# Strided products begun in the prologue, and the weight conversions regrouped, in a fused attention and mixture-of-experts kernel

## The chip, the cores and the metric

The kernel runs on one core of one Trainium2 chip. The metric is the device time of one execution in microseconds (us); the figure for a kernel is the median over its runs. TensorE is called PE, VectorE DVE, ScalarE ACT, GpSimd POOL, and SyncE, which issues the loads, SP.

## The reference, cut to what matters

```python
# attention: 4 batches, 8 heads, 576 positions, head size 64
scores = (q @ k.T) / 8
# heads 0-3: the last 32 positions ("local"); heads 4-7: every 32nd position ("strided")
attn = softmax(where(mask, scores, -1e9)) ; x = attn @ v          # -> x: 2304 x 512
# dense layer
h = x @ w_in                                                      # 512 -> 2048
g = h * sigmoid(1.702 * h)
x = g @ w_out                                                     # 2048 -> 512
# eight experts, two for each token
top2 = two largest of (x @ w_gate + log1p(exp(x @ w_noise)) * noise)
out += weight * (relu(x @ w1[e]) @ w2[e])   for each e in top2
```

## The kernel before, in words

Every fp32 product is made of three: an operand is split into a rounded part ("hi") and its remainder ("lo"), and hi*hi, hi*lo and lo*hi are accumulated in one PSUM bank.

**Attention** is cut into groups. A strided group covers 126 or 72 reordered positions of two heads, a local group 192 positions of two heads. A group passes through all engines: scores on PE (L223 or L238), mask and row minimum on DVE (L186), exponentials on ACT (L191), sums and reciprocals on DVE (L195, L198), scaling on POOL (L200), transposes on PE (L251 or L256) and their copy on ACT (L252 or L257), the product with v on PE (L268 or L278), and last the split of the result into the hi part of `xt` on ACT (L208) and its lo part on DVE (L211).

**The prologue** is the loop that ends before the dense layer. Its step k (0 to 16) issues the scores, mask and exponentials of group k, the reciprocals of group k-1, the transposes of group k-3 and the products with v of group k-4. Groups 0 to 9 are the strided ones of batch 0, groups 10 to 13 the local ones that its first 384 tokens need. `warm` (L890) is a product of ones into a bank that is about to be written; its result is never read.

**The dense layer** runs in slices (c, fc): 384 tokens, 128 hidden units. Slices 0 to 7 are (0, 0) to (0, 7). Slice (c, fc) has a first product (`m1_l1`, L461 to L463: four blocks kc of the 512 inputs, three products each, into bank fc % 2), tanh on ACT (L466), a product on DVE (L470), a split (L475 on ACT, L477 on POOL or DVE), and a second product (`m1_l2`, L487 to L489, nine instructions) that is issued one slice later. Blocks kc 2 and 3 of `xt` come from the strided heads, 0 and 1 from the local ones. In slices 0 to 7 two further attention groups are worked on between the products.

**Conversions.** The weights come as raw 64-bit words, in halves called pieces here: (f, 0) is the half of block f that the first product reads, (f, 1) that of the second. Turning a piece into fp32 takes three DVE instructions (L422, L425, L429), a cast on ACT (L393) and a subtraction on POOL (L394). The cast and the subtraction come one slot after the DVE instructions (a prologue step, or half a slice, is a slot), and only when they have been issued does the load of piece (f+2, s) follow on SP, into the buffer that they free (`w_split` calls `w_raw`; all these loads pass through `chained`, L157, in one order). `CONVAT` lists the prologue steps that convert a piece; each slice converts one in its first half, and slices 0, 2, 4 and 6 one in the second half too (L988). A conversion's first instruction stands ahead of the mask of its step; in the prologue its temporary is PSUM bank 7, later the SBUF tile `cv`.

PE, ACT, DVE and POOL run their instructions in the order in which the code issues them (`manual_schedule`): an instruction that waits holds back all behind it on its engine.

Of the kernel before, what the change touches and what calls it, by code (L numbers as in the profile page):

```python
# [28 lines left out]
CH = 384  # L29
# [5 lines left out]
NG = -(-BAND // RPG)  # L35
# [20 lines left out]
HALFC = NFC // 2  # L56
FIRSTLD = 18
SMALLS = 18
CONVAT = (4, 6, 7, 9, 11, 13)
R_PP = R_LG + 16 * TPC  # L60

XA = (0, 1, 0, 2, 1, 0, 2, 1)
# [45 lines left out]
def tile_kernel(ctx, tc, attL, attS, wm1, wm2, wgn, noise, cst, lst0, out):  # L108
    nc = tc.nc
# [4 lines left out]
    PB = [psum.tile([128, 512], F32, tag=f"pb{i}", name=f"pb{i}") for i in range(8)]  # L114
# [15 lines left out]
    with ExitStack() as main, tc.manual_schedule(engines={mybir.EngineType.PE}):  # L130
# [12 lines left out]
        def third(i):  # L143
            return XT[:, :, :, CH * (i % 3):CH * (i % 3) + CH]

        X = [third(c) for c in range(NCHUNK)]
# [242 lines left out]
        def w_split():  # L389

            for fc, s, w32, o, n in SPLIT.pop(0):
                hi, lo = W1[fc, s]
                nc.scalar.copy(hi[:, o:o + n], w32)  # L393
                nc.gpsimd.tensor_sub(lo[:, o:o + n], w32, hi[:, o:o + n].bitcast(F32))  # L394
                if n < 512:
                    held.pop()
                else:
                    w_raw(fc + 2, s)
            w_small()
            SPLIT.append([])  # L400
            done.append(0)

        def w_step():
            left = 512
            while PIECES and left:
                fc, s, raw, o, n = PIECES[0]
                if n < 512:
                    if len(done) < born[0] + LATE:
                        return
                    born.pop(0)  # L410
                PIECES.pop(0)
                left -= n
                yield from w_bits(fc, s, raw, o, n, PB[7][:, :n].bitcast(I32) if INPS else None)
# [35 lines left out]
                    nc.scalar.mul(p, PB[2 + j], 0.5)  # L449
                PART.append(p)  # L450

        def m1_l1(c, fc, mid, conv, between=None):
            w = W1[fc, 0]
            ps = PB[fc % 2][:, :CH]
            for n, kc in enumerate((2, 3, 0, 1)):
                if n == 2:
                    mid()
                if n == 3 and (c, fc) == (0, 0):
                    finish(0, [5])
                a = slice(128 * kc, 128 * kc + 128)  # L460
                nc.tensor.matmul(ps, w[0][:, a], X[c][:, 0, kc, :], start=(n == 0), stop=False)  # L461
                nc.tensor.matmul(ps, w[0][:, a], X[c][:, 1, kc, :], start=False, stop=False)  # L462
                nc.tensor.matmul(ps, w[1][:, a], X[c][:, 0, kc, :], start=False, stop=(n == 3))  # L463
            t = tmp.tile([128, CH], F32, tag="th", name="th", bufs=1)
            g = tmp.tile([128, 2, CH], F32R, tag="g", name="g")
            nc.scalar.activation(t, ps, AF.Tanh, scale=0.851)  # L466
            next(conv, None)
            if between:
                between()
            nc.vector.scalar_tensor_tensor(t, t, 1.0, ps, op0=OP.add, op1=OP.mult)  # L470
            GT[c, fc] = g
            return t, g
# [410 lines left out]
        upto = [sum(map(len, parts[:k + 1])) for k in range(len(parts))]  # L883
        att = Attention(sum(parts, []), upto[1], upto[1])
# [4 lines left out]
        def warm(bank):  # L889
            nc.tensor.matmul(bank.rearrange("p (t d) -> p t d", d=128), ones,  # L890
                             ones[:, None, :].to_broadcast([128, 4, 128]), start=True, stop=True)
# [8 lines left out]
        w_raw(1, 0)  # L900
        w_raw(1, 1)
        k = 0
        while att.done < upto[0] - REM:
            conv = w_step() if k in CONVAT else iter(())
            next(conv, None)
            if k and not att.nc:
                warm(PB[att.na % 3])
            att.scores([0, 1, 2])
            next(conv, None)
            att.norms(conv, True)  # L910
            if att.done < att.nc:
                warm(PB[5 + att.done % 2])
            att.values([5, 6])
            if k in CONVAT and att.nc < att.ready:
                warm(PB[3 + att.nc % 2])
            att.transposes([3, 4])
            att.exps()
            att.load()
            next(conv, None)
            for _ in conv:  # L920
                pass
            w_split()
            k += 1
# [27 lines left out]
        def finish(c, bank=[7]):  # L951
            while att.done < upto[c]:
                att.exps()
                att.values([7])
                att.norms()
                att.transposes([6])

        seq = [(c, fc) for c, a, b in SEGS for fc in range(a, b)]
        for i, (c, fc) in enumerate(seq):
# [10 lines left out]
            conv = w_step()  # L970
# [14 lines left out]
            for _ in conv:  # L985
                pass
            w_split()
            conv = w_step() if i < HALFC and not i % 2 or i >= SMALLS else iter(())  # L988
            if i < HALFC:
                att.exps()  # L990
                next(conv, None)
# [80 lines left out]
        for h in range(H0, H1):  # L1072
            e, fc = divmod(h, NF2)
# [44 lines left out]
    with tc.tile_pool(name="ovf", bufs=1) as op:  # L1118
        n = nc.values_load(nrow[:, 0:1], min_val=0, max_val=NJ)  # L1119
        with tc.For_i(0, n, 1) as j:  # L1120
# [14 lines left out]
            w = op.tile([128, NF2, 1024], F32, name="ow")  # L1135
            nc.sync.dma_start(w, wm2[bass.ds(e8, NF2)].rearrange("f p n -> p f n"))
            for fc in range(NF2):
                ps = PB[fc % 2][:, :128]
# [79 lines left out]
```

## Time and profile before

| what | value |
|---|---|
| median of 3 runs | 970.48 us (970.12 to 972.08) |
| the profiled execution's own time | 970.01 us |
| its span, first to last instruction | 968.2 us |
| PE busy | 951.5 us (98%) |
| DVE busy | 523.8 us (54%) |
| ACT busy | 387.8 us (40%) |
| POOL busy | 217.2 us (22%) |

The span is 1.8 us shorter than the execution's own time; what lies around it is taken as fixed. The shares are means over stages: in the prologue (up to 35.15 us) and in the dense layer the engines are loaded quite differently, so that single stretches and the order of single instructions have to be read.

### The profile page before, as it was taken

What the parts mean: (1) busy time and instruction counts of PE and PEld (TensorE: products, weight loads), DVE (VectorE), ACT (ScalarE), POOL (GpSimd) and SP (SyncE); (2) the same over time, 40 slices, a digit from 0 to 9 for tenths busy, and PEclk for the clock granted to TensorE, in tenths of its full rate; (3) what the DMA queues carried; (4) which work ended last, traced back from release to release, by engine and by line L of the source; (5) the groups of instructions that cost most, each with busy time, mean ns of one, the idle gap of its engine ahead of it and who ended that gap; (6) DMA issues with size and microseconds to landing.
All of it is one profiled execution on the core that took longest, in us unless ns stands there. A gap on an engine that the chain in (4) does not pass through costs nothing. (4 is left out here: it accounts for less than half of the span.)

```text
span 968.2 us, 15951 instructions
## 1 busy us (share of the span) xinstructions
PE 951.5 (98%) x5706; PEld 839.4 (87%) x5706; DVE 523.8 (54%) x1519; ACT 387.8 (40%) x1031; POOL 217.2 (22%) x206
## 2 busy tenths in 40 slices
PE   8999999999999999999999999999999999999996
PEld 4788899898888889899898988888988989898994
DVE  6889865567645745632666343645546272635511
ACT  6875533244444444223354242333424242433411
POOL 3575231020200200020230512050402204050303
PEclk9999999999999999999999999999999999999998
DMA  9755511061333237301064258276684939576503
GB/s 337 258 191 183 176 60 55 1 134 45 57 102 102 67 69 235 132 1 67 6 198 135 39 141 213 84 178 170 150 216 106 237 117 207 145 174 174 107 1 53
DMA packets 83793, 123.93 MB, mean 128 GB/s; under 512 B 13488, under 2 KB 42800, under 8 KB 83696
## 3 DMA queue, kind: packets, MB, share of 16 engines
q1 hardware_dynamic: 73888, 102.92, 35.5%
q0 software_dynamic: 9824, 19.98, 11.1%
q8 instruction: 45, 0.74, 0.3%
q14 instruction: 36, 0.29, 0.1%
HBM read 93.33 MB, written 29.68 MB: 127 GB/s over the span
## 5 line engine op out<-in xcount | busy, mean ns | idle before, releaser
L832 DVE SCALAR_TENSOR_TENSOR ht<-pb,ht 128x352 fp32r<-128x352 f32 (+2 forms) x126 | 59.1, 472 | 166.8 <-ACT ht L831 166.8
L461 PE MATMUL pb<-xt,w 128*128 128x384 f32 x384 | 132.0, 344 | 0.0
L462 PE MATMUL pb<-xt,w 128*128 128x384 f32 x384 | 129.8, 338 | 0.0
L463 PE MATMUL pb<-xt,w 128*128 128x384 f32 x384 | 129.7, 338 | 0.0
L846 PE MATMUL pb<-w,ht 128*128 128x512 f32 (+1 forms) x315 | 124.2, 394 | 0.2 <-ACT ht L831 0.2
L831 ACT ACTIVATE ht<-pb 128x352 fp32r<-128x352 f32 (+2 forms) x126 | 52.8, 423 | 176.7 <-PE pb L829 175.9
L864 POOL DMA_INDIRECT out<-y,el x40 | 63.1, 1578 | 268.8 <-ACT y L863 239.8
L847 PE MATMUL pb<-w,ht 128*128 128x512 f32 (+1 forms) x315 | 123.4, 392 | 0.0
L848 PE MATMUL pb<-w,ht 128*128 128x512 f32 (+1 forms) x315 | 123.3, 392 | 0.0
L487 PE MATMUL pb<-w,g 128*128 128x512 f32 x288 | 118.3, 411 | 0.3 <-DVE part L447 0.2
L470 DVE SCALAR_TENSOR_TENSOR th<-th,pb 128x384 f32<-128x384 f32 x96 | 52.9, 551 | 112.0 <-ACT th L466 111.9
L489 PE MATMUL pb<-w,g 128*128 128x512 f32 x288 | 113.2, 393 | 0.0
L488 PE MATMUL pb<-w,g 128*128 128x512 f32 x288 | 112.6, 391 | 0.0
L656 POOL DMA_INDIRECT lst<-pay,si x36 | 35.7, 992 | 326.8 <-DVE si L653 285.3
L681 DVE TENSOR_TENSOR w<-raw,w 128x512 fp32r<-128x512 f32 x128 | 85.4, 689 | 30.7 <-ACT w L680 29.0
L466 ACT ACTIVATE th<-pb 128x384 f32<-128x384 f32 x96 | 47.0, 489 | 132.1 <-PE pb L463 124.6
L680 ACT CAST w<-raw 128x512 fp32r<-128x512 f32 x128 | 76.2, 619 | 39.3 <-DMA raw<-wm 36.4
L827 PE MATMUL pb<-xt,w 128*128 128x352 f32 (+1 forms) x256 | 84.1, 329 | 0.0
L829 PE MATMUL pb<-xt,w 128*128 128x352 f32 (+1 forms) x256 | 83.5, 326 | 0.0
L828 PE MATMUL pb<-xt,w 128*128 128x352 f32 (+1 forms) x256 | 83.5, 326 | 0.0
L461 PEld LDWEIGHTS pb<-xt,w 128*128 128x128 f32 x384 | 72.2, 188 | 4.8 <-issue 1.0
L462 PEld LDWEIGHTS pb<-xt,w 128*128 128x128 f32 x384 | 72.1, 188 | 3.8 <-DVE xt L211 0.2
(194 smaller groups left out, 1916.6 us busy)
## 6 DMA issues: line engine op xcount, KB each, us to landing
raw<-wm SPq DMA_DIRECT2D x136, 256.0 KB, 3.1
area<-wm SPq DMA_DIRECT2D x28, 512.0 KB, 5.1
xs<-g SPq DMA_DIRECT2D x24, 256.0 KB, 3.7
out<-zero SPq DMA_DIRECT2D x7, 768.0 KB, 4.7
att<-attS SPq DMA_DIRECT2D x20, 253.0 KB, 5.0
qk<-attL SPq DMA_DIRECT2D x16, 304.0 KB, 4.3
tr<-xs SPq DMA_DIRECT2D x24, 176.0 KB, 3.8
att<-attL SPq DMA_DIRECT2D x8, 496.0 KB, 8.2
```

The source lines that it names most:

```text
L461: nc.tensor.matmul(ps, w[0][:, a], X[c][:, 0, kc, :], start=(n == 0), stop=False)
L462: nc.tensor.matmul(ps, w[0][:, a], X[c][:, 1, kc, :], start=False, stop=False)
L463: nc.tensor.matmul(ps, w[1][:, a], X[c][:, 0, kc, :], start=False, stop=(n == 3))
L487: nc.tensor.matmul(o, g[:, 0, a], w[0], start=((c, fc) in FIRST), stop=False)
L488: nc.tensor.matmul(o, g[:, 0, a], w[1], start=False, stop=False)
L489: m = nc.tensor.matmul(o, g[:, 1, a], w[0], start=False, stop=((c, fc) in LAST))
L681: nc.vector.tensor_sub(w[:, 1, o], raw, w[:, 0, o].bitcast(F32))
L827: nc.tensor.matmul(ps, w[:, 0, a], x[:, 0, kc, :], start=(kc == 0), stop=False)
L828: nc.tensor.matmul(ps, w[:, 0, a], x[:, 1, kc, :], start=False, stop=False)
L846: nc.tensor.matmul(o, hi, w[:, 0, 512:], start=(fc == 0), stop=False)
L847: nc.tensor.matmul(o, hi, w[:, 1, 512:], start=False, stop=False)
L848: m = nc.tensor.matmul(o, lo, w[:, 0, 512:], start=False, stop=(fc == NF2 - 1))
```

## The change

The first six products of slice 0 (blocks kc 2 and 3) are issued in prologue steps 15 and 16, where they stand in place of two `warm` products; the first six of slice 1 are issued in slice 0, ahead of what is left of the prologue's attention (`finish`). The block kc 0 of slice 0 moves behind that rest. The prologue's last two conversions move from steps 11 and 13 to steps 10 and 12. The second conversions of slices 0 and 6 go, slice 3 gets one, and those of slices 2 and 4 stay; a piece that was converted in slice 0's second half is now converted in slice 1, and all later pieces follow half a slice to a slice later. `warm` ahead of the transposes now runs in every step from 4 to 12. Scores of the groups after the fourteenth use banks 1 and 2 alone, since bank 0 holds the started products.

```diff
--- before.py
+++ after.py
@@ -56,7 +56,10 @@
 HALFC = NFC // 2
 FIRSTLD = 18
 SMALLS = 18
-CONVAT = (4, 6, 7, 9, 11, 13)
+NS = 2 * NG
+AHEAD1 = (0, 1)
+TWICE = (2, 3, 4)
+CONVAT = (4, 6, 7, 9, 10, 12)
 R_PP = R_LG + 16 * TPC
 
 XA = (0, 1, 0, 2, 1, 0, 2, 1)
@@ -449,18 +452,31 @@
                     nc.scalar.mul(p, PB[2 + j], 0.5)
                 PART.append(p)
 
-        def m1_l1(c, fc, mid, conv, between=None):
+        def m1_products(c, fc, kcs):
+
             w = W1[fc, 0]
             ps = PB[fc % 2][:, :CH]
-            for n, kc in enumerate((2, 3, 0, 1)):
-                if n == 2:
-                    mid()
-                if n == 3 and (c, fc) == (0, 0):
-                    finish(0, [5])
+            for kc in kcs:
                 a = slice(128 * kc, 128 * kc + 128)
-                nc.tensor.matmul(ps, w[0][:, a], X[c][:, 0, kc, :], start=(n == 0), stop=False)
+                nc.tensor.matmul(ps, w[0][:, a], X[c][:, 0, kc, :], start=(kc == 2), stop=False)
+                yield
                 nc.tensor.matmul(ps, w[0][:, a], X[c][:, 1, kc, :], start=False, stop=False)
-                nc.tensor.matmul(ps, w[1][:, a], X[c][:, 0, kc, :], start=False, stop=(n == 3))
+                yield
+                nc.tensor.matmul(ps, w[1][:, a], X[c][:, 0, kc, :], start=False, stop=(kc == 1))
+                yield
+
+        def m1_l1(c, fc, mid, conv, between=None):
+            ps = PB[fc % 2][:, :CH]
+            if c or fc not in AHEAD1:
+                for _ in m1_products(c, fc, (2, 3)):
+                    pass
+            mid()
+            if (c, fc) == (0, 0):
+                for _ in m1_products(0, 1, (2, 3)):
+                    pass
+                finish(0, [5])
+            for _ in m1_products(c, fc, (0, 1)):
+                pass
             t = tmp.tile([128, CH], F32, tag="th", name="th", bufs=1)
             g = tmp.tile([128, 2, CH], F32R, tag="g", name="g")
             nc.scalar.activation(t, ps, AF.Tanh, scale=0.851)
@@ -900,18 +916,23 @@
         w_raw(1, 0)
         w_raw(1, 1)
         k = 0
+        ahead = m1_products(0, 0, (2, 3))
         while att.done < upto[0] - REM:
             conv = w_step() if k in CONVAT else iter(())
             next(conv, None)
             if k and not att.nc:
                 warm(PB[att.na % 3])
-            att.scores([0, 1, 2])
+            att.scores([0, 1, 2] if att.na < upto[0] + 1 else [2, 1])
             next(conv, None)
             att.norms(conv, True)
             if att.done < att.nc:
-                warm(PB[5 + att.done % 2])
+                if att.done > NS:
+                    for _ in range(2 if att.done == NS + 1 else 4):
+                        next(ahead)
+                else:
+                    warm(PB[5 + att.done % 2])
             att.values([5, 6])
-            if k in CONVAT and att.nc < att.ready:
+            if CONVAT[0] <= k <= CONVAT[-1] and att.nc < att.ready:
                 warm(PB[3 + att.nc % 2])
             att.transposes([3, 4])
             att.exps()
@@ -985,7 +1006,7 @@
             for _ in conv:
                 pass
             w_split()
-            conv = w_step() if i < HALFC and not i % 2 or i >= SMALLS else iter(())
+            conv = w_step() if i in TWICE or i >= SMALLS else iter(())
             if i < HALFC:
                 att.exps()
                 next(conv, None)
```

PE at the end of the prologue, before (steps 15 and 16 and the start of slice 0; pb_63 is bank 0, pb_64 bank 1 and so on, `ones` are the `warm` products, `w_0_124` is weight block 0):

```order
L223 MATMUL pb_63<-att 128x96 x3
L890 LDWEIGHTS ones
L890 MATMUL pb_69<-ones 128x512
L268 MATMUL pb_69<-att 64x64 x6
L251 MATMUL pb_66<-cs,att 96x128 x3
L223 MATMUL pb_64<-att 128x96 x3
L890 LDWEIGHTS ones
L890 MATMUL pb_68<-ones 128x512
L268 MATMUL pb_68<-att 64x64 x6
L251 MATMUL pb_67<-cs,att 96x128 x3
L461 MATMUL pb_63<-xt,w_0_124 128x384
```

The same place with the change (L461, L463 and L465 are the three products of a block, L271 the product with v, L254 the transposes):

```order
L226 MATMUL pb_64<-att 128x96 x3
L461 MATMUL pb_63<-xt,w_0_124 128x384
L463 MATMUL pb_63<-xt,w_0_124 128x384
L271 MATMUL pb_69<-att 64x64 x6
L254 MATMUL pb_66<-cs,att 96x128 x3
L226 MATMUL pb_65<-att 128x96 x3
L465 MATMUL pb_63<-xt,w_0_124 128x384
L461 MATMUL pb_63<-xt,w_0_124 128x384
L463 MATMUL pb_63<-xt,w_0_124 128x384
L465 MATMUL pb_63<-xt,w_0_124 128x384
L271 MATMUL pb_68<-att 64x64 x6
L254 MATMUL pb_67<-cs,att 96x128 x3
```

Two and four products have taken the place of a `warm` each, and the products of slice 1 (weight block 1, into bank 1) follow at once.

DVE in prologue step 10, before (L186 is the mask of one of three tiles, the first row the end of step 9):

```order
L211 TENSOR_TENSOR xt<-pb_69,xt 128x7x18
L186 ISA att,stats<-pb_64,cs 128x96
L186 ISA stats 128x1
...
L195 TENSOR_REDUCE stats<-stats 72x2
L198 RECIPROCAL stats<-stats 72x2
L211 TENSOR_TENSOR xt<-pb_68,xt 128x7x18
L422 TENSOR_SCALAR pb_70<-area 128x512
```

The same step with the change:

```order
L214 TENSOR_TENSOR xt<-pb_69,xt 128x7x18
L425 TENSOR_SCALAR pb_70<-area 128x512
L189 ISA att,stats<-pb_64,cs 128x96
L189 ISA stats 128x1
...
L428 SCALAR_TENSOR_TENSOR pb_70<-area,pb_70 128x512
L432 SCALAR_TENSOR_TENSOR area<-area,pb_70 128x512
L198 TENSOR_REDUCE stats<-stats 72x2
L201 RECIPROCAL stats<-stats 72x2
```

The three conversion instructions, which read `area`, the raw piece, now stand in step 10, the first of them ahead of its masks; before, the first one opened step 11.

DVE in slice 0, between the last instruction of its first conversion and the lo part of group 15, before:

```order
L429 SCALAR_TENSOR_TENSOR area<-area,cv 128x512
L422 TENSOR_SCALAR cv<-area 128x512
L425 SCALAR_TENSOR_TENSOR cv<-area,cv 128x512
L195 TENSOR_REDUCE stats<-stats 128x3
L429 SCALAR_TENSOR_TENSOR area<-area,cv 128x512
L198 RECIPROCAL stats<-stats 128x3
L211 TENSOR_TENSOR xt<-pb_70,xt 128x192
```

With the change:

```order
L432 SCALAR_TENSOR_TENSOR area<-area,cv 128x512
L198 TENSOR_REDUCE stats<-stats 128x3
L201 RECIPROCAL stats<-stats 128x3
L214 TENSOR_TENSOR xt<-pb_70,xt 128x192
```

The three instructions of the second conversion are gone from this place.

## Rows read from the trace of the kernel before

**Rows 1.** Page, part 1: engine, busy us (share of the span), instructions.

```profile
PE 951.5 (98%) x5706; PEld 839.4 (87%) x5706; DVE 523.8 (54%) x1519; ACT 387.8 (40%) x1031; POOL 217.2 (22%) x206
```

**Rows 2.** Windows: stretch, length, busy of PE, PEld, DVE, ACT, POOL, granted clock, DMA share, GB/s.

```profile
23.38:35.00 11.62, 10.18 (x101) 7.11 (x100) 10.58 (x67) 10.45 (x48) 7.34 (x9) 1.00 1.01 388
...
52.69:59.22 6.53, 6.53 (x45) 5.30 (x44) 6.14 (x21) 4.29 (x16) 2.86 (x4) 1.00 0.67 236
59.22:65.23 6.01, 6.01 (x41) 4.86 (x40) 4.61 (x19) 4.82 (x17) 5.72 (x7) 1.00 0.36 116
```

**Rows 3.** Timeline, DVE, prologue: start, duration, instruction (masks of steps 10 and 12, a conversion).

```profile
23.38 0.25 DVE L186 CUSTOM_DVE_ANT_0 att<-pb,cs 128x96 f32<-128x96 f32 x1
...
24.50 0.69 DVE L422 TENSOR_SCALAR pb<-area 128x512 int32<-128x512 int32 x1
...
27.55 0.25 DVE L186 CUSTOM_DVE_ANT_0 att<-pb,cs 128x96 f32<-128x96 f32 x1
```

**Rows 4.** Timeline, SP's queue: issues of raw pieces, in three short stretches.

```profile
15.90 0.33 SPq L157 DMA_DIRECT2D area<-wm  x1
...
21.47 0.33 SPq L157 DMA_DIRECT2D area<-wm  x1
...
59.76 0.33 SPq L157 DMA_DIRECT2D area<-wm  x1
```

**Rows 5.** DMA issues of 15.5 to 16.3 and 21.3 to 21.8 us: size, issue to landing.

```profile
area<-wm SPq DMA_DIRECT2D x1, 512.0 KB, 8.5
...
area<-wm SPq DMA_DIRECT2D x1, 512.0 KB, 6.6
```

**Rows 6.** Timeline, ACT, 32 to 39 us; idle time before an instruction and its releaser bracketed.

```profile
32.03 0.38 ACT L191 ACTIVATE att<-att,stats 128x96 f32<-128x96 f32 x1 [0.28 <-DVE stats L186]
...
33.12 0.60 ACT L393 CAST w<-area 128x512 fp32r<-128x512 f32 x1
33.63 0.31 ACT L208 CAST xt<-pb 128x192 fp32r<-128x192 f32 x1
...
34.21 0.38 ACT L191 ACTIVATE att<-att,stats 128x96 f32<-128x96 f32 x1
...
37.51 0.32 ACT L208 CAST xt<-pb 128x192 fp32r<-128x192 f32 x1 [0.45 <-PE pb L268]
...
38.93 0.49 ACT L466 ACTIVATE th<-pb 128x384 f32<-128x384 f32 x1 [0.48 <-PE pb L463]
```

**Rows 7.** Timeline, PE, slices 0 and 1.

```profile
42.18 0.34 PE L462 MATMUL pb<-xt,w 128*128 128x384 f32 x1
...
43.95 0.34 PE L463 MATMUL pb<-xt,w 128*128 128x384 f32 x1
44.80 0.57 PE L268 MATMUL pb<-att 96*64 96x64 f32 x12 [0.51 <-DVE xt L211]
...
46.03 0.48 PE L487 MATMUL pb<-w,g 128*128 128x512 f32 x1
```

**Rows 8.** Timeline, DVE, slice 0: second conversion and lo part of group 15.

```profile
42.44 0.43 DVE L422 TENSOR_SCALAR cv<-area 128x512 int32<-128x512 int32 x1
...
44.32 0.33 DVE L211 TENSOR_TENSOR xt<-pb,xt 128x192 fp32r<-128x192 f32 x1
```

**Rows 9.** Timeline, PE, second product of slice 8.

```profile
92.11 0.39 PE L488 MATMUL pb<-w,g 128*128 128x512 f32 x1
92.35 0.40 PE L489 MATMUL pb<-w,g 128*128 128x512 f32 x1
92.94 0.50 PE L487 MATMUL pb<-w,g 128*128 128x512 f32 x1 [0.19 <-DVE part L447]
```

**Rows 10.** Timeline, DVE, slice 4: conversion of piece (6, 0) and what follows.

```profile
63.00 0.54 DVE L422 TENSOR_SCALAR cv<-area 128x512 int32<-128x512 int32 x1
...
65.23 0.56 DVE L470 SCALAR_TENSOR_TENSOR th<-th,pb 128x384 f32<-128x384 f32 x1 [1.05 <-ACT th L466]
```

**Rows 11.** Tile view of the raw pieces, 55 to 80 us: issue to landing.

```profile
DMA to landing us min/median/max: 3.5/3.7/5.8
```

## The prediction, made before the changed kernel was run

> **What bounds the kernel now.** I read the page first: PE is busy for 98% of the span [rows 1], so almost everywhere only the removal of PE work, or of PE's waits, can bring time. Then the windows of the stretches that the change touches. From 23.38 to 35 us, the end of the prologue, DVE is busy for 10.58 of 11.62 us, PE for 10.18 with its `warm` products counted, and the DMA engines for all of it [rows 2]. So PE's time there isn't what sets the end: DVE's order of work does, and ACT behind it. The timeline of DVE gives the length of a prologue step: step 10, without a conversion, lasts from 23.38 to 24.50, 1.12 us; step 11, with one, from 24.50 to 27.55, 3.05 us; DVE doesn't wait in them [rows 3]. The timeline of ACT shows who takes over at the end: from 32.03 us on, exponentials, cast, hi part and copy stand shoulder to shoulder, 1.09 us for the exponentials of a group (32.03 to 33.12), 0.51 for the cast, 0.58 for hi part and copy (33.63 to 34.21), until ACT waits for PE at 37.51 and for slice 0's first product at 38.93 [rows 6]. From slice 1 on PE runs without a break, but for a wait on DVE's lo part ahead of 44.80 [rows 7] and one at 92.94 [rows 9].
>
> **What moving the products is worth.** A product of 384 columns takes 1.77 us / 10 = 0.177 us in a row of them (42.18 to 43.95) [rows 7]. Twelve are 2.1 us of PE work that leave slices 0 and 1 and go where PE waits anyway. In steps 15 and 16 six of them (1.06 us) replace two `warm`s. The cover is ACT: its period there is 1.09 + 0.58 = 1.67 us a step [rows 6], while PE has some 1.4 us of scores, products with v and transposes; only the four products of step 16 go beyond that, by about 0.1 to 0.4 us, and I charge 0.1, because the transposes after them have slack until ACT comes to their copy. Without the cover the six would cost 1.06 us less two warms. The extra `warm`s in steps 5, 8, 10 and 12 and the changed score banks I cost at nothing: in those steps PE waits for DVE and ACT, and the banks' last readers are a step or more back. If that cover were gone, four products of about 0.23 us would cost 0.9.
>
> **What moving the conversions costs.** The sum of DVE work up to the end of step 13 is the same; so that alone doesn't delay step 14. But the raw piece of the conversion that now opens step 10 was issued at 15.90 us [rows 4] and took 8.5 us to land [rows 5], at 24.40. Step 11, which used it before, opened at 24.50 and found it there with 0.1 us to spare. Step 10 opens at 23.38 [rows 3]. DVE then stands at its first conversion instruction for 1.0 us, with the masks of groups 10 on behind it. The load can't come earlier: POOL frees its buffer no sooner than before. The next piece, issued at 21.47 with 6.6 us to land [rows 4, 5], is there at 28.1; step 12 then opens at about 23.38 + 1.05 + 3.05 + 1.15 = 28.6, so no wait. The bounds for this wait are 0, if the landing under the same load varies, and 1.1 us; I take 1.05.
>
> Does the delay reach PE? Masks of step 13 start at about 31.6 (step 13 opens 1.05 + 3.05 + 1.15 + 3.05 after 23.38, at 31.7). The exponentials follow 0.3 us on, about 31.95. Then ACT has 1.09 + 0.51 for the cast, which stood behind group 14 and now stands behind group 13, then three times 0.58 + 1.09 for hi part, copy and exponentials of groups 14 to 16: 31.95 + 1.60 + 5.01 = 38.56. There the hi part of group 13 starts, which was at 37.51 [rows 6]: 1.05 us later. The products of block kc 1 need it; block kc 0, now behind `finish`, covers the wait for it. With the 0.1 of PE, tanh of slice 0 comes 1.1 us later, at 40.0 in place of 38.93. So slice 0's six early products give nothing back: the end of slice 0's first product hangs on group 13, not on PE.
>
> **Slices 0 and 1.** Behind that tanh PE has six products less (1.06 us) and DVE one conversion less. Before, PE waited 0.51 us for DVE ahead of 44.80 [rows 7], because the second conversion, from 42.44, pushed the lo part of group 15 to 44.32 [rows 8]. Without it the sums of group 17 follow at 42.44, and the lo part 0.35 us later, at 42.8, 1.5 us earlier; with the delay of 1.1 it stands at 43.9, 0.4 earlier than before. The second of PE's products of slice 1 started at 42.18 [rows 7]; with the delay and six of them the row of them is through at 42.18 + 1.1 + 5 x 0.177 = 44.2, while the lo part is done by 43.9 + 0.33 = 44.2 [rows 8]: both end together, where before DVE came 0.5 us after PE. The first `m1_l2`, at 46.03 before [rows 7], comes 0.4 us earlier, at 45.6. I carry that 0.4 through slices 1 to 8, which are PE's own pace.
>
> **Slices 2 to 8.** Three slices in a row now convert two pieces. A slice with two keeps DVE busy for 6.14 of 6.53 us, one with one for 4.61 of 6.01 [rows 2]; a third conversion pair of about 1.6 us fits slice 3 with next to nothing left. And pieces are loaded closer to their use: the piece (6, 0) is issued when a subtraction frees its buffer at the end of slice 2, at 59.76 [rows 4], and slice 4 asks for it at 63.00 [rows 10], 3.24 us later. Landings in this stretch take 3.5 to 5.8 us [rows 11]. This issue stands alone, so I take the median, 3.7: DVE waits 0.5 us, and behind that instruction it idles 1.05 us for the tanh of slice 4 anyway [rows 10]. At 5.8 it would be 2.6 - 1.05 = 1.5 us late, part of it PE's; bounds 0 and 1.5, value 0. Of the later weights the last, (15, 1), becomes the tightest; I cost it at nothing, and at one subtraction on POOL at most. On the gaining side, slice 6 loses a conversion, and DVE reaches the copy at L447 earlier. PE waited for it ahead of 92.94: from 92.35 to 92.94 is 0.59 us, and a product's start follows the last by 0.24 (92.11 to 92.35) [rows 9]. That is 0.35 us; bounds 0 and 0.35, and I take all, since DVE's backlog there is shorter than the conversion removed.
>
> **The sum.** -0.4 at the first `m1_l2`, -0.35 at L447, 0 elsewhere: -0.75 us. Against the profiled execution's 970.01 us that gives 969.3. Its median is 0.47 higher (970.48), which would give 969.7; I say 969.5.
>
> **A rule of the Trainium skill against a row.** The row gives 8.5 us for 512 KB in a stretch where the DMA engines are busy all the time, and 3.5 us for the fastest of the same size later [rows 5, 11]. The Trainium skill, page "DMA: Bandwidth & Descriptors", section "Anatomy of one DMA — SWDGE (gpsimd) path", gives a fixed 2.0 us and bytes at 436 GB/s, which for this size is an estimate of 3.2 us; its fit was made on another path of issue. By that rule the piece would be there by 19.1 us, DVE would not wait, and the sum would be that of the first rival; the trace agrees with it for the lone transfer, not for the one that counts here.
>
> **The rivals.**
> *The prologue isn't delayed.* If the piece lands before 23.4 us, as a queue with less in it would let it, ACT's chain starts 1.05 us earlier, tanh of slice 0 stands at 38.9 to 39.0, and all that slice 1's products and DVE's missing conversion save comes through: 0.4 + 1.05 = 1.45 us, up to 1.7 where PE's end takes over, and 0.35 at L447: -1.8 to -2.1, 967.9 to 968.7 with the median's offset. For it: landings vary from 6.6 to 8.5 in the same stretch [rows 5]. Against it: the engines are saturated and the issues before it are untouched.
> *DVE becomes the bound in slices 2 to 4.* If DVE needs 6.5 to 6.6 us for each slice with two conversions where PE takes 6.4, up to 0.6 us are lost: -0.2, 969.8 to 970.2. For it: 6.14 busy us of 6.53 [rows 2] leave 0.4 for waits. Against it: in a slice that had two, PE was busy for all of the 6.53 us [rows 2].
> *Slower: the conversions run out of raw pieces.* The place is the conversion of (6, 0) in slice 4, ahead of the tanh product on DVE. With a landing L, DVE is late by L - 3.24 - 1.05 [rows 4, 10]; it decides at L = 4.3 us, and at the 8.5 of the prologue [rows 5] it is 4.2 us: +4.2 - 0.75 = +3.45 if all of it reaches PE, 973.5 to 973.9. For it: that stretch has landings of 5.8. Against it: DMA is busy there for 36% of the time [rows 2], not 100%.
>
> **Chances, time and range.** A difference under 0.2%, 1.9 us, can't be told from no change here. Forecast (-0.75, with the smaller bounds -1.3 to +0.5) 0.57; no delay 0.17; DVE as the bound 0.18; raw pieces late 0.08. Faster by over 0.2%: most of the second case, 0.13, and 0.02 of the first. Slower: the last, 0.08. Within: 0.77. The range reaches from the second case, 968.0, to the forecast with the wait for raw pieces at its bound of 1.5 us and the spread of the runs above their median (972.08 against 970.48), 971.6.
>
> **What would show it.** Right: DVE idles about 1 us ahead of the conversion that opens step 10, released by the load of `area`; tanh of slice 0 at 40 us; the first L503 (the former L487) at 45.6; no wait ahead of slice 8's second product; the rest the same to 0.2 us. Wrong: no such idle time, and tanh at 39; a wait of DVE for `area` in slices 3 to 5 with PE waiting behind it; a granted clock below the 1.00 of these windows, since fewer `warm`s run; or weights late in slices 22 to 24.

## The result and the profile after

The changed kernel takes 975.96 us (median of 6 runs, 973.97 to 976.54), the kernel before 970.44 us in the same comparison: 1.0052 times as long, 95% interval 1.0041 to 1.0063. It is 5.5 us slower, where 0.75 us less was forecast, and outside the range of 968.0 to 971.6. The profiled execution took 975.71 us with a span of 973.9 us, 5.7 us more than that of before in both.

Where these 5.7 us arise is read from one event per slice, the start of the first `m1_l2` product of slice k (in slice k + 1 of the loop). After minus before it is +2.93 us for slice 0, +2.88 for slice 2, +3.62 for slice 3, +4.84 for slices 4 to 7, +4.35 from slice 9 on, +4.37 still for slice 20, and +5.70 for slice 24 and all that follow in the stage. So there are four places: the prologue with slice 0 (+2.93: tanh of slice 0 comes 4.54 us late, and 1.61 us of that are won back by the first `m1_l2`), the conversions of slices 3 and 4 (+1.95), the copy at the old L447 (-0.48) and the weights of slices 22 to 24 (+1.33); together +5.73.

The page of the changed kernel, part 1, answers to [rows 1]; lines of the changed file are higher by 3 below the table of constants (conversion L425 to L432, cast L396, POOL's subtraction L397) and by 16 in the slices (`warm` L906, tanh L482, products of `m1_l2` L503 to L505); those of `m1_l1` are L461, L463 and L465 now:

```profile
PE 954.3 (98%) x5707; PEld 841.5 (86%) x5707; DVE 521.5 (54%) x1519; ACT 388.8 (40%) x1031; POOL 216.7 (22%) x206
```

PE is busy for 2.8 us more with one instruction more: its work did not grow, it ran slower somewhere. The windows of the end of the prologue (columns as in [rows 2]; the third number from the end is the granted clock) show where:

```profile
23.06:26.50 3.44, 3.44 (x28) 2.47 (x28) 2.20 (x12) 1.65 (x8) 1.26 (x2) 1.00 1.02 416
26.50:28.40 1.90, 0.07 (x2) 0.00 (x0) 1.69 (x6) 1.67 (x7) 0.21 (x1) 1.00 1.02 417
...
29.00:31.00 2.00, 2.00 (x12) 1.70 (x10) 1.99 (x10) 2.00 (x11) 2.00 (x3) 0.50 0.78 306
31.00:33.00 2.00, 2.00 (x12) 1.27 (x11) 1.79 (x10) 1.09 (x7) 1.30 (x2) 0.50 0.83 266
33.00:35.40 2.40, 2.40 (x20) 1.71 (x20) 1.41 (x13) 2.00 (x8) 1.06 (x3) 0.50 0.69 201
35.40:37.00 1.60, 1.60 (x11) 1.34 (x11) 0.61 (x4) 1.22 (x5) 1.58 (x2) 0.88 0.79 295
```

PE does almost nothing from 26.5 to 28.4 us, and behind that the granted clock is 0.50, the 1.2 GHz level, for 6.4 us, in which PE is busy without a break. The timeline shows what stood ahead, and the other three places (start, duration, instruction, idle time before it with its releaser):

```profile
16.38 0.33 SPq L160 DMA_DIRECT2D area<-wm  x1
...
25.11 0.69 DVE L425 TENSOR_SCALAR pb<-area 128x512 int32<-128x512 int32 x1 [1.14 <-DMA area<-wm]
...
28.37 0.38 PE L906 MATMUL pb<-ones 128*128 128x512 bf16 x1 [1.83 <-DVE xt L214]
...
43.47 0.49 ACT L482 ACTIVATE th<-pb 128x384 f32<-128x384 f32 x1 [0.57 <-PE pb L465]
...
48.96 0.47 PE L503 MATMUL pb<-w,g 128*128 128x512 f32 x1
...
58.19 0.43 DVE L425 TENSOR_SCALAR cv<-area 128x512 int32<-128x512 int32 x1
...
64.11 1.73 POOL L397 TENSOR_TENSOR w<-area,w 128x512 fp32r<-128x512 f32 x1
...
64.72 1.40 DVE L425 TENSOR_SCALAR cv<-area 128x512 int32<-128x512 int32 x1
...
68.06 0.35 PE L281 MATMUL pb<-att 72*64 72x72 f32 x4 [0.57 <-DVE xt L214]
...
71.76 1.74 POOL L397 TENSOR_TENSOR w<-area,w 128x512 fp32r<-128x512 f32 x1
...
72.38 1.40 DVE L425 TENSOR_SCALAR cv<-area 128x512 int32<-128x512 int32 x1
...
75.79 0.44 PE L281 MATMUL pb<-att 126*64 126x126 f32 x4 [1.10 <-DVE xt L214]
...
97.18 0.39 PE L505 MATMUL pb<-w,g 128*128 128x512 f32 x1
97.41 0.40 PE L503 MATMUL pb<-w,g 128*128 128x512 f32 x1
...
163.86 1.49 POOL L397 TENSOR_TENSOR w<-raw,w 128x256 fp32r<-128x256 f32 x2 [5.81 <-ACT w L396]
...
164.15 0.19 PEld L503 LDWEIGHTS pb<-w,g 128*128 128x128 f32 x1 [0.16 <-ACT w L396]
...
165.41 0.50 PE L504 MATMUL pb<-w,g 128*128 128x512 f32 x1 [0.76 <-POOL w L397]
```

In order: VectorE waits for the raw piece of step 10, as forecast; its lo part comes late, PE stands for 1.83 us, and tanh of slice 0 comes at 43.47, 4.54 us after that of [rows 6] and not 1.1. Slice 2's second conversion opens with an instruction of 0.43 us; that of slices 3 and 4 takes 1.40 us, each time while POOL's subtraction of 1.73 us runs, and PE then waits for VectorE's lo part (0.57 and 1.10 us). At the copy of slice 8 PE no longer waits (97.18 to 97.41, where [rows 9] had 0.59 us between starts). And the last weights, cast and subtraction of (15, 1), come after PE asks for them. In the kernel before, POOL was through with the last of them at 156.02 + 0.74 = 156.76 us, 2.83 us ahead of their first use:

```profile
156.02 0.74 POOL L394 TENSOR_TENSOR w<-raw,w 128x256 fp32r<-128x256 f32 x1 [1.33 <-ACT w L393]
...
159.59 0.39 PE L487 MATMUL pb<-w,g 128*128 128x512 f32 x1
```

### The profile page after: what moved, and what is told of

Its sections match the earlier page's. It is cut to its first block, busy times and chain, and to the rows that moved or that the text cites. A ratio compares the mean times of both kernels' runs of the same rounds, so it can differ in the third digit from the quotient of the medians.

```text
span 973.9 us, 15961 instructions
## 1 busy us (share of the span) xinstructions
PE 954.3 (98%) x5707; PEld 841.5 (86%) x5707; DVE 521.5 (54%) x1519; ACT 388.8 (40%) x1031; POOL 216.7 (22%) x206
## 5 line engine op out<-in xcount | busy, mean ns | idle before, releaser
L461 PE MATMUL pb<-xt,w 128*128 128x384 f32 x384 | 131.9, 344 | 0.0
L465 PE MATMUL pb<-xt,w 128*128 128x384 f32 x384 | 129.7, 338 | 0.0
L463 PE MATMUL pb<-xt,w 128*128 128x384 f32 x384 | 129.6, 337 | 0.0
L503 PE MATMUL pb<-w,g 128*128 128x512 f32 x288 | 118.3, 411 | 0.0
L505 PE MATMUL pb<-w,g 128*128 128x512 f32 x288 | 113.2, 393 | 0.0
L482 ACT ACTIVATE th<-pb 128x384 f32<-128x384 f32 x96 | 47.0, 490 | 136.2 <-PE pb L465 125.5
L461 PEld LDWEIGHTS pb<-xt,w 128*128 128x128 f32 x384 | 72.1, 188 | 4.6 <-issue 1.0
L463 PEld LDWEIGHTS pb<-xt,w 128*128 128x128 f32 x384 | 72.1, 188 | 3.6
```

Of the source, the lines that this page charges most:

```text
L461: nc.tensor.matmul(ps, w[0][:, a], X[c][:, 0, kc, :], start=(kc == 2), stop=False)
L503: nc.tensor.matmul(o, g[:, 0, a], w[0], start=((c, fc) in FIRST), stop=False)
L505: m = nc.tensor.matmul(o, g[:, 1, a], w[0], start=False, stop=((c, fc) in LAST))
```

## The experiments

Four theories: **1**, VectorE's wait in step 10 leaves PE idle and its clock falls; **2**, two conversions in three slices in a row run into POOL's subtractions; **3**, the early products by themselves gain; **4**, the one conversion fewer in slices 0 to 7 makes the last weights late. The table gives for each kernel how much later (or earlier) than before the first `m1_l2` product of a slice starts in its profiled execution, and its time against the runs of before on the same chip. Ahead of slice 9 stand what the prologue and the conversions do; from 9 to 20 nothing should move; from 20 to 24 the last weights come in. Each row is one execution, and the first raw piece, at which VectorE begins, was there between 9.39 and 10.71 us in them: a few tenths between two kernels at slice 0 mean little, steps along a row are exact to some 0.05.

| kernel | slice 0 | 3 | 4 | 8 | 9 | 20 | 24 | median us (before) | ratio, 95% |
|---|---|---|---|---|---|---|---|---|---|
| before, start in us | 46.03 | 65.45 | 71.84 | 91.79 | 97.46 | 147.12 | 163.75 | | |
| after | +2.93 | +3.62 | +4.84 | +4.83 | +4.35 | +4.37 | +5.70 | 975.96 (970.44) | 1.0041 to 1.0063 |
| E1 | -1.67 | -0.98 | +0.22 | +0.22 | -0.26 | -0.24 | +1.99 | 972.81 (970.75) | 1.0009 to 1.0027 |
| E2 | +2.85 | +2.83 | +2.84 | +2.84 | +2.84 | +2.83 | +2.84 | 973.89 (970.75) | 1.0022 to 1.0043 |
| E3 | +5.52 | +5.52 | +5.52 | +5.52 | +5.51 | +5.50 | +5.51 | 973.60 (970.75) | 1.0021 to 1.0041 |
| E4 | -0.15 | +0.57 | +1.78 | +1.75 | +1.27 | +1.30 | +3.84 | 974.39 (970.75) | 1.0023 to 1.0048 |
| E5 | +1.01 | +1.71 | +2.93 | +2.90 | +2.42 | +2.46 | +3.77 | 973.79 (970.42) | 1.0024 to 1.0051 |
| E6 | +0.42 | +0.37 | +0.38 | +0.38 | +0.36 | +0.36 | +0.37 | 970.20 (970.42) | 0.9988 to 1.0006 |
| E7 | -1.74 | -1.79 | -1.79 | +1.72 | +2.72 | +2.98 | +3.00 | 974.09 (970.42) | 1.0028 to 1.0055 |
| E8 | -2.10 | -2.15 | -2.14 | -2.15 | -2.63 | -2.59 | -1.08 | 968.64 (970.42) | one run |
| E9 | -1.70 | -1.59 | -1.57 | +1.44 | +2.09 | +2.08 | +2.09 | 973.75 (970.59) | 1.0025 to 1.0051 |
| E10 | -1.82 | -1.12 | -1.10 | +1.18 | +1.80 | +1.80 | +1.81 | 972.44 (970.59) | 1.0011 to 1.0028 |
| E11 | -1.79 | -1.09 | +0.13 | +0.85 | +1.49 | +1.49 | +1.50 | 972.94 (970.59) | one run |
| E12 | -1.30 | -1.24 | -0.43 | -0.44 | -0.92 | +0.60 | +0.61 | 971.12 (971.06) | 0.9991 to 1.0009 |

**E1 and E2, one half of the change taken back.** E1 is the kernel after with the prologue's conversions in their old steps, E2 with the old slices converting twice.

```diff
E1  -CONVAT = (4, 6, 7, 9, 10, 12)
    +CONVAT = (4, 6, 7, 9, 11, 13)
E2  -TWICE = (2, 3, 4)
    +TWICE = (0, 2, 4, 6)
```

> The kernel after, with the prologue's conversions back in steps 4, 6, 7, 9, 11, 13; the early products and the slices 2, 3, 4 with two conversions stay. Theory 1 (the wait of VectorE for the raw piece in step 10 leaves TensorE without work, and its granted clock then falls): no wait for area of about 1 us in the prologue, granted clock 1.00 from 24 us on, first m1_l2 at 44.6 to 45.6 us in place of 48.96, and with the late slices unchanged 971.3 to 972.2 us. Rival (the clock falls because products stand where warm products stood): the clock is 0.50 again somewhere between 29 and 36 us, and the time stays at 975 to 976 us.

> The kernel after, with two conversions in slices 0, 2, 4, 6 as before; the prologue stays as after. Theory 2 (in slices 3 and 4 a second pair of conversions on VectorE meets POOL's subtraction, 1.9 us in all, and one conversion fewer in slices 0 to 7 makes the last weights late, 1.3 us): tanh of slice 5 comes 2.9 us or so after that of before as slice 3's does, not 5.4; no step of 1.3 us ahead of slice 25; TensorE waits 0.5 us more in slice 0; total 972.5 to 973.5 us. Rival (the losses in slices 3 to 5 come from the slower start of the prologue, not from the conversions): 975 to 976 us as after.

E1: no wait for `area` in step 10, the clock 1.00 from 24 us on, the first `m1_l2` at 44.36, 4.6 us earlier than after. (The edit also lets one `warm` more run, in step 13.) Theory 1's forecast holds; its rival falls, for in E1 the products stand where warm products stood, and the clock does not fall. The steps of slices 3 and 4 (+0.74 and +1.20, from -1.72 at slice 2) and of slices 20 to 24 (+2.23) are all still there.

E2 is the mirror image: behind slice 0 not one slice loses anything, so its rival falls. Its 2.85 us lie ahead of that. Tanh of slice 0 comes at 41.79 (+2.86), and from there to the first `m1_l2` it takes 7.09 us, as before (7.10; after 5.49), because the second conversion is back in slice 0 and PE waits for VectorE's lo part, 1.56 us where 0.5 more were expected:

```profile
47.66 0.57 PE L271 MATMUL pb<-att 96*64 96x64 f32 x12 [1.56 <-DVE xt L214]
```

Up to that conversion E2 is the program of after, whose tanh comes at 43.47. In E2 the granted clock is 0.55 and 0.60 in the windows of 28 to 30 and 30 to 32 us and 1.00 again from 32 on; in after it stays low until past 35. So how long the slow stretch lasts differs between executions of the same instructions. Behind slice 0 the two halves of the change cost time at different places, independently. The medians of E1 and E2 lie 0.4 to 0.6 us above the intervals expected for them.

**E3 and E4, one half of the change alone.** E3 is the kernel before with the new steps of the conversions, E4 with the new slices converting twice.

```diff
E3  -CONVAT = (4, 6, 7, 9, 11, 13)
    +CONVAT = (4, 6, 7, 9, 10, 12)
E4  -            conv = w_step() if i < HALFC and not i % 2 or i >= SMALLS else iter(())
    +            conv = w_step() if i in (2, 3, 4) or i >= SMALLS else iter(())
```

> The kernel before with the prologue's conversions in steps 4, 6, 7, 9, 10, 12 alone. Theory 1: VectorE waits about 1.1 us for area in step 10, TensorE then stands for 1.5 to 2 us, its clock is 0.50 in the stretch behind it, first m1_l2 at 48.5 to 49.5 us (46.03 before), 973 to 974.5 us. Rival (the wait costs only itself, the clock needs the products in place of the warm products too): clock 1.00, first m1_l2 at 47.1 us, 971.5 us. The prediction's own step: tanh of slice 0 at 40.0 us.

> The kernel before with two conversions in slices 2, 3, 4 alone. Theory 2: the wait of TensorE ahead of 44.80 goes (0.5 us) and the one ahead of 92.94 (0.35 us), 1.9 us are lost in slices 3 and 4 and 1.3 us ahead of slice 25: 972.4 to 973.2 us. Rival (three such slices in a row fit, as the prediction had it): 969.4 to 969.8 us.

E3 has every warm product of before and no early product, and still shows the wait (0.90 us on VectorE), 2.36 us without work on PE, and then this in its windows:

```profile
26.00:28.00 2.00, 0.00 (x0) 0.00 (x0) 1.79 (x8) 1.92 (x9) 0.05 (x1) 0.99 1.03 419
28.00:30.00 2.00, 1.88 (x9) 0.79 (x8) 1.90 (x14) 1.67 (x8) 2.00 (x3) 0.50 1.00 407
...
36.00:38.00 2.00, 2.00 (x11) 1.43 (x9) 0.69 (x4) 1.56 (x7) 1.17 (x2) 0.50 0.66 223
38.00:40.00 2.00, 2.00 (x25) 1.64 (x26) 1.11 (x10) 1.18 (x5) 0.67 (x1) 0.95 0.91 269
```

The clock is 0.50 for ten microseconds: the first `m1_l2` comes 5.52 us late, at 51.55, where 48.5 to 49.5 were expected; the median, 973.60, lies in its interval. The ten runs reach from 972.01 us (mean granted clock 0.994 of the whole span) to 976.41 (0.991, as in the profiled run, 975.67). The mean clock does not order them all: one of 975.68 has 0.994. E4 confirms theory 2 at its place (+0.76 and +1.21 us in slices 3 and 4, from -0.19 at slice 2, and -0.48 at slice 9); its weights are 2.54 us late, not 1.3, so its time is 1.2 us above what was expected. The prediction's view, that three such slices fit, would have given 969.4 to 969.8.

**E5, the wait stays, PE gets something to do.** Ten warm products more in step 10 of the kernel after, ahead of what waits for VectorE.

```diff
             att.scores([0, 1, 2] if att.na < upto[0] + 1 else [2, 1])
+            if k == 10:
+                for _ in range(10):
+                    warm(PB[att.na % 3])
             next(conv, None)
```

> The kernel after, with ten more warm products in step 10, right behind the scores and ahead of everything that waits for VectorE (2.1 us of TensorE's time). Theory 1 (the clock falls because TensorE stands still behind VectorE's wait for area): the clock is 1.00 from 24 us on although VectorE waits as before; first m1_l2 at 45.3 to 46.2 us in place of 48.96; with the later losses of after (1.95, -0.48, 1.34) 972.3 to 973.5 us. Rival (VectorE's wait itself is the whole delay, or the clock falls for another reason): first m1_l2 at 48.5 us or later, 975 us.

The timeline and, below, two windows of E5:

```profile
25.00 0.69 DVE L425 TENSOR_SCALAR pb<-area 128x512 int32<-128x512 int32 x1 [1.94 <-DMA area<-wm]
...
28.27 0.38 PE L906 MATMUL pb<-ones 128*128 128x512 bf16 x1 [1.29 <-DVE xt L214]
...
32.76 0.37 ACT L194 ACTIVATE att<-att,stats 128x96 f32<-128x96 f32 x1 [0.62 <-DVE stats L189]
...
40.05 0.32 ACT L211 CAST xt<-pb 128x192 fp32r<-128x192 f32 x1
...
41.55 0.49 ACT L482 ACTIVATE th<-pb 128x384 f32<-128x384 f32 x1 [0.57 <-PE pb L465]
...
47.04 0.47 PE L503 MATMUL pb<-w,g 128*128 128x512 f32 x1
```

```profile
28.00:30.00 2.00, 1.73 (x15) 1.16 (x14) 1.90 (x12) 1.59 (x8) 1.91 (x3) 1.00 0.94 380
30.00:32.00 2.00, 1.76 (x16) 1.23 (x15) 1.85 (x9) 2.00 (x11) 1.61 (x2) 1.00 0.59 201
```

VectorE waits even longer (1.94 us, since its step opens earlier), PE's idle time shrinks from 1.83 to 1.29 us, the clock stays at 1.00, and the first `m1_l2` comes at 47.04, 1.92 us earlier than after. That is the clock's share in these two executions; between the medians, each against before on its own chip, it is 2.15 us (5.52 and 3.37). It can be smaller: tanh of slice 0 comes at 41.55 in E5 and at 41.79 in E2. What is left was expected 0.8 us smaller than it is; the point-by-point part says why.

**E6, the early products alone**, both tables as before, the code of after.

```diff
-CONVAT = (4, 6, 7, 9, 10, 12)
+CONVAT = (4, 6, 7, 9, 11, 13)
-TWICE = (2, 3, 4)
+TWICE = (0, 2, 4, 6)
```

> The early products alone: prologue's conversions in steps 4, 6, 7, 9, 11, 13 and two conversions in slices 0, 2, 4, 6, all as before. Theory 3 (the products are worth about 1.5 us as soon as nothing delays the prologue): first m1_l2 at 44.3 to 44.7 us (46.03 before), this lead kept through slice 25, 1.3 to 1.7 us below before. Rival (the second conversion in slice 0 holds the lo part of group 15 up, so that TensorE only waits for it longer): first m1_l2 at 45.5 to 46.0, 0 to 0.5 us below before.

The rival is right: ratio 0.9997. The timeline of E6, VectorE's second conversion in slice 0 and PE:

```profile
42.87 0.43 DVE L425 TENSOR_SCALAR cv<-area 128x512 int32<-128x512 int32 x1
...
44.06 0.69 DVE L432 SCALAR_TENSOR_TENSOR area<-area,cv 128x512 int32<-128x512 int32 x1
...
44.75 0.33 DVE L214 TENSOR_TENSOR xt<-pb,xt 128x192 fp32r<-128x192 f32 x1
...
45.23 0.57 PE L271 MATMUL pb<-att 96*64 96x64 f32 x12 [1.58 <-DVE xt L214]
```

PE is through with slice 1's products sooner and waits 1.58 us for the lo part, where it waited 0.51 in [rows 7]: the six products saved (1.06 us) turned into 1.07 us more of waiting. (The 0.42 us at slice 0 are there at tanh already, 39.37 against 38.93; the first raw piece was there at 10.71, in before at 9.98.) Free of such starts is the time from tanh of slice 0 to the first `m1_l2`: 7.10 us in before, 7.08 in E6, 6.52 in E4, which only drops that conversion, and 5.49 in E1, which has both. So the products alone give nothing there, the dropped conversion alone 0.58 us, and both together 1.61. (E4's -0.15 in the table hides most of its 0.58: its first raw piece came 0.42 us later than before's.)

**E7, E9, E10, E11 and E12, other slices with two conversions**, the prologue's conversions in their old steps, the rest as after.

```diff
all  -TWICE = (2, 3, 4)
E7   +TWICE = (2, 4, 6, 8)
E9   +TWICE = (1, 3, 5, 7)
E10  +TWICE = (2, 3, 5, 7)
E11  +TWICE = (2, 3, 4, 7)
E12  +TWICE = (1, 3, 4, 14)
```

> The kernel after with the prologue's conversions in their old steps and two conversions in slices 2, 4, 6 and 8: as many as before up to slice 8, and never in two slices in a row. Theories 1 to 3: first m1_l2 at 44.3 us, the lead of 1.7 us kept through slice 25, no step in slices 3, 4 and 21 to 25: 1.5 to 2.2 us below before. Rival (slice 8, whose conversion stands in another place, or the pieces that now come later, give the lead back): 0 to 1 us below before, with a step in slices 5 to 9 or 21 to 25.

> The kernel after with the prologue's conversions in their old steps and two conversions in slices 1, 3, 5 and 7: never two such slices in a row, and the 13th conversion, which slice 6 needs at its start, in the first half of slice 4 as before. Theories 1 to 3: first m1_l2 at 44.3 us, the lead of 1.7 us kept, 0.48 us more behind slice 8, no step in slices 21 to 25: 1.5 to 2.3 us below before. Rival (slice 1, from which six products are taken too, becomes VectorE's as slice 0 did): a step of 0.7 to 2 us at the second m1_l2, 0 to 1 us below before.

> As the run before, with the two conversions in slices 2, 3, 5 and 7. Theory 2 (each slice whose second conversion follows a slice with two loses time to POOL's subtraction): one step, 0.74 us in slice 3, in place of the 0.74 and 1.20 of slices 3 and 4; 0.48 back behind slice 8; no step in slices 21 to 25; 1.2 to 1.6 us below before. Rival (the loss belongs to the third conversion pair in a row, not to the second): no step in slice 3, 2.2 us below before.

> The kernel after with the prologue's conversions in their old steps and a fourth slice with two conversions, the seventh. Theory 4 (the step of 1.3 to 2.2 us in slices 21 to 25 comes from the one conversion fewer in slices 0 to 7): steps of 0.74 and 1.20 us in slices 3 and 4 as in the first of these runs, no step in slices 21 to 25, span within 0.4 us of that of before. Rival (the late weights come from something else, as POOL's order): the step of 2.2 us stays, span 1.9 us above before.

> The kernel after with the prologue's conversions in their old steps and two conversions in slices 1, 3, 4 and 14: three in slices 0 to 4, so that the 13th and the 15th conversion stand in the first halves of slices 4 and 5 as in after, only one pair of slices in a row, and the missing fourth where VectorE has time. Theories 1 to 4: first m1_l2 at 44.3 us (1.7 to 1.8 below before), one step of 0.74 us in slice 4 and none in slice 3, no wait for weights in slices 6 and 7, 0.48 back behind slice 8, no step in slices 21 to 25: 1.2 to 1.7 us below before. Rival (the step in slice 4 is 1.2 us because of what the slice has to do, not of its place in the row; or weights are late again): 0 to 1 us below before, with TensorE waiting for w in slices 4 to 7.

Misses as to the time, all five, but each settles something. Without two such slices in a row, the steps of slices 3 and 4 are gone (E7: -1.79 in both; E9: -1.59 and -1.57, so the rival for slice 1 falls too). With one pair there is one step, in the second slice of the pair: 0.74 us in slice 3 of E10, 0.81 in slice 4 of E12; the rival of E10 falls. As many conversions as before up to slice 7 (E9, E10, E11), and nothing is lost from slice 20 to 24; the rival of E11 falls, and theory 4 holds. What takes the gain away lies elsewhere. Two timelines, of E7 and of E9:

```profile
72.34 1.73 POOL L397 TENSOR_TENSOR w<-area,w 128x512 fp32r<-128x512 f32 x1
...
74.12 0.44 PE L465 MATMUL pb<-xt,w 128*128 128x384 f32 x1 [0.66 <-POOL w L397]
```

```profile
81.01 0.45 PE L465 MATMUL pb<-xt,w 128*128 128x384 f32 x1 [1.77 <-POOL w L397]
```

In E7 slices 6 and 7 (0.66, then 1.19 and 1.04 us), in E9 (and E10, 1.09 us) slice 7 find their weights not yet converted or subtracted. These three have two slices with two conversions ahead of slice 5; before, after, E11 and E12 have three there and no such wait. And a second conversion in slice 7 costs 0.75 us at slice 8 and 0.64 at slice 9 (E11), one in slice 14 1.5 us (E12). There VectorE's own instructions meet POOL again, in the timeline of E12:

```profile
125.36 2.95 POOL L397 TENSOR_TENSOR w<-area,w 128x512 fp32r<-128x512 f32 x2 [3.42 <-ACT w L396]
...
125.53 1.63 DVE L493 TENSOR_TENSOR g<-th,g 128x384 fp32r<-128x384 f32 x1
...
127.22 0.50 PE L505 MATMUL pb<-w,g 128*128 128x512 f32 x1 [1.19 <-DVE g L493]
```

The tanh product took 1.63 us beside POOL's subtractions (0.55 for that of the slice before), and PE waited 1.19 us for it. E12 ends even with before.

**E8, POOL's subtractions of slices 2 to 4 taken out** (E1 with zeros written to those lo halves, so that part of the weights is left out of the result).

```diff
-                nc.gpsimd.tensor_sub(lo[:, o:o + n], w32, hi[:, o:o + n].bitcast(F32))
+                if ZERO[0]:
+                    nc.gpsimd.memset(lo[:, o:o + n].bitcast(F32), 0.0)
+                else:
+                    nc.gpsimd.tensor_sub(lo[:, o:o + n], w32, hi[:, o:o + n].bitcast(F32))
```

> The kernel after with the prologue's conversions in their old steps, and POOL's subtractions that fall in slices 2 to 4 replaced by zeros written to the lo halves (so these halves are left out of the result). Theory 2 (what is lost in slices 3 and 4 is VectorE's conversion instruction running against POOL's subtraction): the first instruction of the second conversion takes 0.43 us in slices 3 and 4 in place of 1.39 and 1.40, and the 0.74 and 1.20 us that slices 3 and 4 lose shrink to 0.3 or less each. Rival (VectorE has too much to do there in any case): the two losses stay above 0.5 us each.

VectorE does the same three conversions in a row; the timeline of E8 (slices 3 and 4; L429 is the former L425):

```profile
59.06 0.53 POOL L398 MEMSET w<- 128x512 f32 x1
...
59.71 0.43 DVE L429 TENSOR_SCALAR cv<-area 128x512 int32<-128x512 int32 x1
...
66.28 0.43 DVE L429 TENSOR_SCALAR cv<-area 128x512 int32<-128x512 int32 x1
```

0.43 us where after had 1.40, and both steps are gone (-2.15 throughout). The work on VectorE fits, as the prediction had it; what did not fit is its meeting with POOL.

## Why the prediction was wrong, step by step

**The wait in step 10** was forecast at 1.05 us and is 1.14 in the run after; in place and cause it is right. That the size fits is in part luck: the step opened at 23.97, not 23.38, and the piece came later too, and in the other kernels that ask for it there the wait is 0.90 (E3), 1.80 (E2) and 1.94 us (E5). The landing was taken as that of [rows 5], 8.5 us, or 24.40; VectorE had the piece at 25.11, 25.00, 24.89 and 24.86 us in the four (after, E5, E2, E3), up to 9.5 us after its issue (15.49 to 25.00 in E5).

**"Does the delay reach PE?"** is the step that failed. It followed the chain to its end on ACT and did not ask what PE does meanwhile: it stands for 1.83 us, and its granted clock then falls to 0.50, the 1.2 GHz level. That is 1.92 us (after against E5). A granted clock below 1.00 stood among the signs of error, but with the wrong reason: not fewer warm products (after runs 29 of them in all, before 28), but idle time behind VectorE (E3 has all of before's and its clock falls too).

**The chain on ACT** was right in its links and short in two. In E5, which has no fallen clock, the exponentials of group 13 come at 32.76, not 31.95 (+0.81: 0.57 because VectorE has the piece at 25.00 and not 24.43, the rest in small parts of the steps behind it). From there the forecast adds 1.60 + 5.01 and has the hi part at 39.37; it comes at 40.05 (+0.68): ACT waits for PE at 38.03 (0.24 us, the rest in shorter gaps around it), and PE, with its extra products, is busy for all of 36 to 42 us there; 0.1 was charged. With the forecast's 1.05 that makes 2.54, the hi part's delay against [rows 6], and tanh follows 1.50 us later (1.42 before). From the forecast's -0.4 at the first `m1_l2`, 0.81 + 0.68 - 0.1 leads to +0.99; E5 measured +1.01.

**Slices 0 and 1**: the first `m1_l2` was to come 5.6 us after tanh (7.10 before). It came 5.49 us after it, in E1 and E5 as well. Right, and with it the working by which PE and VectorE end together: E6 and E4 show that either cause alone holds most of the gain back. That slice 0's products give nothing back ahead of tanh held too: in E1, without the delay, tanh comes at 38.87, 0.06 us earlier than before. The 1.67 us that E1 gains at the first `m1_l2` are the size of the first rival.

**Slices 2 to 8**: no price for three slices with two conversions, 0.6 us at most in the rival; 1.95 measured, 1.97 in E4. The working added busy times as if an instruction had one duration. It named the wrong limit too: VectorE's time suffices (E8), but each second conversion in the slice behind another one opens while POOL subtracts the piece converted a half slice earlier. The Trainium skill, page "SBUF — State Buffer", section "Who interferes with whom", says that VectorE and GpSimd share one pair of ports, that an instruction which needs it waits until the other's is done, whole, and that it depends on which issued first. The trace agrees in the order: POOL's instruction ends at 64.11 + 1.73 = 65.84, VectorE's, which began second, at 64.72 + 1.40 = 66.12, 0.28 us behind it (alone it takes 0.43; spans on POOL are rough). Looked up ahead, this page would have asked for the neighbours of each instruction that moves.

**Raw pieces late**: VectorE never waits for `area` in slices 3 to 5. The slower rival did not happen. **The copy at L447** gave 0.48 us, 0.35 were forecast.

**The last weights** were costed at nothing; they cost 1.33 us after, 1.31 in E5, 2.23 in E1, 2.54 in E4 and 1.51 in E8, all with one conversion fewer in slices 0 to 7. With the fourth one back in slices 0 to 14 (E2, E7, E9 to E12) nothing is lost there. In before the last subtraction ended 2.83 us ahead of its use; in after it ends at 163.86 + 1.49 = 165.35, 8.59 us later, and only 4.37 of that is the lag that the kernel has at slice 20 anyway. The other 4.22 are about the length of a slice there (4.16), more than there was to spare. What sets the size of the loss is not shown; how early PE arrives does not order it (at slice 20 the five stand at +4.37, +2.46, -0.24, +1.30 and -2.59).

**The rule on transfers** (the Trainium skill, page "DMA: Bandwidth & Descriptors", section "Anatomy of one DMA — SWDGE (gpsimd) path") gave 3.2 us as an estimate; with the DMA engines busy all the time it was 8.5 to 9.5 us here, and the trace decides.

So the sum reads: -0.4 + 1.4 (landing and PE) + 1.9 (clock) + 1.95 + 1.33 - 0.48 = +5.7, in place of -0.4 - 0.35. The upper end of the range was added up wrongly as well: 969.5, the wait of 1.5 and the spread of 1.6 us make 972.6, not 971.6. The measured time lies above both.

What stays open: why the clock fell behind some idle stretches and not behind others of like length (below) and for how long, what sets the size of the loss at the last weights, and whether a placing exists that keeps E1's lead. None of the five tried does.

## What to carry to other kernels

When one engine is made to wait, look at what TensorE does in that time: if it stands, the clock may fall, and a wait of one microsecond can cost several (0.90 us on VectorE in E3, 5.5 us at the first `m1_l2`); ten `warm` products put into the gap took 1.9 us off here. Work that is moved on VectorE takes the duration of its new neighbours on POOL, not that of its old place. And work dropped from a pipeline's early slots shifts all that follows: check the last user, not only the next. And where two things hold PE back at the same place, take both away together: one alone gave nothing here, the other 0.58 of 1.61 us.

## What the runs showed of the hardware that was not expected

Idle times of PE of 1.83 us (after), 2.34 (E2) and 2.36 us (E3) were followed by the 0.50 clock for 6.4, over 3 and some 10 us, in which PE was busy almost throughout. Around 17 us PE idles in every one of these kernels, waiting for the same load: 1.32 us in after and 1.43 in E2, and the clock falls to 0.50, from about 19 to 22 us and 18 to 21; 1.26 us in before, 1.31 in E5, 1.32 in E10 and 1.33 in E9, and it stays at 1.00. So, from one execution to the next, idle times of 1.32 and 1.33 us went either way here.

The same VectorE instruction (tensor_scalar, 128 x 512, input and output in SBUF) took 0.43 us alone and 1.40 us beside POOL's two-input subtraction, and the tensor_tensor of the tanh product 0.55 and 1.63 us.
